# Dealing a weight conversion out over the slots of the first batch, and moving reciprocals one slot later

## The chip, the cores and the metric

The kernel runs on one core of a Trainium2 chip. The metric is the device time of one execution in microseconds (us), taken as the median of several runs. Engines are named as in the profile: PE is TensorE (matmuls and transposes), PEld its weight loads, DVE is VectorE, ACT is ScalarE, POOL is GpSimd, SP is SyncE (DMA issue). L405 is line 405 of the kernel.

## The reference

Attention with a threshold, followed by a two-layer network with an exact GELU. There are 8 batches of 8 heads, 576 tokens and 64 elements a head; the network has a width of 512 and 2048 hidden units.

```python
scores = scale * np.matmul(q, k.transpose(0, 1, 3, 2))
thresh = np.max(scores, axis=-1, keepdims=True) - tau
scores = np.where(scores >= thresh, scores, -1000000000.0)
scores = scores - np.max(scores, axis=-1, keepdims=True)
attn = np.exp(scores)
attn = attn / (np.sum(attn, axis=-1, keepdims=True) + 1e-09)
attn_out = np.matmul(attn, v)
...
x = attn_out.transpose(0, 2, 1, 3).reshape(B * S, H * D)
h = x @ w_in
g = 0.5 * h * (1.0 + erf(h * inv_sqrt2))
return g @ w_out
```

q, k and v are float32. The two weights are float64 and reach the kernel as 64-bit words, so that the kernel must make float32 of them by itself.

## The kernel before, in words

**Pairs and slots.** The attention works on pairs of heads, p = 0 to 31, four pairs a batch (`HP`). The 576 rows of a head are cut into four chunks of 128 and one of 64; the last chunks of both heads share one tile. One pair and one chunk make a slot. The list `slots` gives their order, and the main loop at L1050 takes one slot n after another. In the first batch (`BATCH`, slots 0 to 19; `EARLY` is 4 pairs) the order is special: slots 0 to 7 take chunks 0 and 1 of the four pairs, slots 8 to 19 take chunks 2, 3 and 4 of pair 0, then of pair 1, and so on. So slots 10, 13, 16 and 19 are the last, half-sized chunks.

**Order.** The schedule is manual. Every engine executes its own instructions in the order in which the program emits them[...]. What the loop emits earlier stands earlier in the queue of its engine.

**A slot of the first batch** emits, in this order:

- `scores` (L393): four or eight matmuls into two PSUM tiles `sc`. There are only two such tiles, so the scores of a slot wait until L424 of the slot before has read them.
- `softmax_head`: for each head, the negated maximum `nmx` (DVE, L405), the threshold `thr` (POOL, L406), the exponential `p` (ACT, L408).
- `turn_qk_early` in slots 0, 2 and 4: transposes of the next pair's q and k (PE L309), copied by ACT.
- `weigh_v` and `divide_early` for what is in `due`: p x v (PE, L527), its copy (ACT, L537); the reciprocal sums spread to columns by matmul (PE, L446), their copy (ACT, L448), the product on POOL (L454). `due` holds chunks of earlier slots, two slots late at the soonest.
- `fill`: matmuls of the network's first layer (PE, L603), from slot 10 on, as many as a fixed goal for each slot asks; `need > converted[0]` holds back those whose weights are not yet converted.
- `turn_p_early` of the slot before: transposes of p (PE, L339), copied by ACT (L346, L355; L350, L359 for the last chunk). For a last chunk this comes after the next item but one.
- `convert(0, least)`: at least one step of the conversion, up to 700 ns of steps where i is 4.
- `softmax_tail`: threshold, product and row sums (DVE, L424), and 1e-9 added to the sums (POOL, L427).
- transposes of q and k for the second batch in slot 17 (`turn_qk`, L375 to L381; the q there is scaled by ACT, L363).
- `convert(ns)`: steps of the conversion worth ns.
- `invert`: the reciprocal of the slot's sums (DVE, L433), which waits for L427.

**The conversion.** The weights come in 32 pieces of 128 x 512 numbers. For each piece ACT makes two values (L201, `power`; L202) and DVE takes three steps (L209, L211, L214), booked by the generator `conversions` at 340, 720 and 640 ns. A piece's two ACT instructions are emitted when an earlier piece ends, so that up to two pieces are `ahead`. `convert` keeps a debt: it adds ns and takes steps until the debt is used up. The end of a piece also issues the load of another piece (L183, on POOL). The raw words lie in tiles that are used by the attention only later (`turned_p`) and in free slots of `xall`.

The main loop gives

```python
convert(0 if n == 0 else 2000 if n < 3 else 3800 if n < BATCH - 1 else 1e9)
if early:
    invert(p, i)
```

which is 2000 ns in slots 1 and 2, 3800 ns in slots 3 to 18, and all that is left in slot 19. The 32 pieces are booked at 54.4 us in all.

**After the first batch** the attention of the other batches runs in the same loop, with its own way of transposing p on DVE, and with more of the network filled in between; then the last ten blocks of 256 tokens are done by `last_blocks`. None of this is touched.

Of the kernel before, what the change touches and what calls it, by code (L numbers as in the profile page):

```python
# [18 lines left out]
def kernel(  # L19
# [37 lines left out]
    EARLY = HP  # L57
# [128 lines left out]
    def conversions():  # L186

        vec = nc.vector
        ahead = []
        while raws or ahead:
            if raws:
                dst, raw, slot = raws.pop(0)
                lo, hi = (raw.rearrange("p (f w) -> p f w", w=2)[:, :, i] for i in range(2))
                power = gp.tile([P, PIECE], U32, tag="g", name="power")  # L200
                nc.scalar.activation(power.bitcast(FP32), hi.bitcast(FP32), AF.Copy, bias=0.0, scale=2.0 ** -112)  # L201
                nc.scalar.activation(dst.bitcast(U32), lo, AF.Copy, bias=0.0, scale=2.0 ** -29)  # L202
                ahead.append((dst, hi, power, slot))
                yield 0
            if len(ahead) == LATER and converted[0] == len(pieces) - LATER:
                yield None
            if len(ahead) == 2 or not raws:
                dst, hi, power, slot = ahead.pop(0)
                vec.tensor_scalar(power, power, 3, 0x7FFFFFF8, op0=ALU.logical_shift_left, op1=ALU.bitwise_and)  # L209
                yield 340  # L210
                vec.scalar_tensor_tensor(power, hi, 0x80000000, power, op0=ALU.bitwise_and, op1=ALU.bitwise_or)  # L211
                x_free.extend(slot)
                yield 720
                vec.tensor_tensor(dst.bitcast(U32), power, dst.bitcast(U32), op=ALU.add)  # L214
                load_piece()
                converted[0] += 1
                yield 640
# [3 lines left out]
    def convert(ns, least=0):  # L221

        if conv["steps"] is None:
            conv["steps"] = conversions()
        conv["debt"] += ns
        while conv["debt"] > 0 or least > 0:
            took = next(conv["steps"], None)
            if took is None:
                return
            conv["debt"] -= took  # L230
            least -= took
# [152 lines left out]
    def scores(p, i):  # L384
        s = st[p]
        n = 1 if i == NC else 2
        sc = s["sc", i] = [ps.tile([P, 2, 512], FP32, tag="sc", name="sc", bufs=2) for _ in range(n)]
        for h in range(2):
            for e in range(n):
                rows = slice(0, P) if i == NC else slice(e * D, (e + 1) * D)  # L390
                lhsT = s["q_tail"] if i == NC else s["qT"][rows, i * P:(i + 1) * P]
                at = h * HALF + (TAIL if p < EARLY and e == 0 else 0)
                nc.tensor.matmul(  # L393
                    sc[e][:, h, 0:HALF], lhsT=lhsT, rhs=s["kT"][rows, at:at + HALF], start=True, stop=True)

    def softmax_head(p, i):

        s = st[p]
        n = len(s["sc", i])
        nmx = small.tile([P, 2], FP32, tag="nmx", name="nmx")  # L400
        thr = s["thr", i] = small.tile([P, 2], FP32, tag="thr", name="thr")
        w = s["p", i] = work.tile([P, 2 * S], FP32, tag="p", name="p")
        for e in range(n):
            sc = s["sc", i][e][:, :, 0:HALF]
            nc.vector.tensor_reduce(nmx[:, e:e + 1], sc, axis=AXIS.XY, op=ALU.max, negate=True)  # L405
            nc.gpsimd.tensor_scalar(  # L406
                thr[:, e:e + 1], nmx[:, e:e + 1], -1.0, tau_eff, op0=ALU.mult, op1=ALU.subtract)
            nc.scalar.activation(  # L408
                w[:, e * S:(e + 1) * S].rearrange("p (h s) -> p h s", h=2), sc, AF.Exp, bias=nmx[:, e:e + 1], scale=1.0)
# [20 lines left out]
    def invert(p, i):  # L430

        den = st[p]["sum", i]
        nc.vector.reciprocal(den, den)  # L433
# [129 lines left out]
    def gelus(left):  # L563


        while len(late) > left:
            g, j, hT = late.pop(0)
            t = gp.tile([P, 2, TOK], FP32, tag="g", name="g")
            if hold[0]:
                nc.scalar.copy(t, hT)  # L570
                held.append((g, j, t))
            else:
                gelu(g, j, t, hT)
# [107 lines left out]
    def weights_first():  # L681
        room = tail["room"] = early_end.enter_context(tc.tile_pool(name="wsum", bufs=1, side="right", reuse_waits="tile"))
        tail["s"] = room.tile([P, 4, 2, 2, P], FP32, name="s_out")
        tail["ss"] = room.tile([P, 4, 3, P], FP32, name="s_in")
        tail["sp"] = room.tile([P, 3, 4, P], FP32, name="s_plain")
        tail["t"] = room.tile([P, 4, 2, HD], FP32, name="t_out")
        w_in_sums(vec, 0)
# [338 lines left out]
    BATCH = HP * SLOTS  # L1026
# [23 lines left out]
    for n in range(len(slots) + WEIGH + 1):  # L1050
        p, i = slots[n] if n < len(slots) else divmod(n, SLOTS)
        early = p < EARLY
        last = slots[n - 1] if 0 < n <= len(slots) else None
        if p < NP:
            scores(p, i)
            softmax_head(p, i)
            if p < HP - 1 and i == 0:
                turn_qk_early(p + 1)
        elif n == len(slots):
            early_end.close()  # L1060
            weights_first()
        gelus(0)
        if n == BATCH:
            gelus_held()
        table()
        for args in due:
            weigh_v(*args)
            divide_early(*args)
        due = []
        if p > EARLY and i == WEIGH:  # L1070
            for lo, hi in (0, WIDE), (WIDE, S):
                weigh_v(p - 1, lo, hi)
            if p == NP:
                divide(p - 1)
        owed += (goal(n) - goal(n - 1)) * BLK_NS * (PARTS[i] if not early and p < NP else 1.0)
        if early:
            fill(owed, tokens)
            owed = 0.0
            table()
        if last and last[0] < EARLY and last[1] < NC:  # L1080
            turn_p_early(*last)
        if early and n > 2:
            convert(0, 700 if i == NC else 1)
        if p < NP:
            softmax_tail(p, i)
        if p < NP and not early:
            turn_p(p, i)
        if p < NP and not early:
            if i == 2:
                regroup(p, 1)  # L1090
            if i > 2:
                regroup(p, i)
            if i == NC:
                divisors(p)
        if last and last[0] < EARLY and last[1] == NC:
            turn_p_early(*last)
        if p < 2 and i == 0:
            for _ in range(2):
                load_piece()
            load_v_early(p + 2)  # L1100
        if p == 1 and i == NC:
            load(HP)
        if n == BATCH - 3:
            load(HP + 1)
        if n == BATCH:
            for t in pd_tail + [turned_p[:, e, h, :, :] for e in range(2) for h in range(2)]:
                nc.gpsimd.memset(t[:, NB:4 * KR, :], 0.0)
        if EARLY < p < NP and i == DIVIDE:
            divide(p - 1)
        if p >= HP and i == 1 and p + 2 < NP:  # L1110
            loads = load_steps(p + 2)
        if p >= HP:
            next(loads, None)
        if p >= HP and i == 1 and p + 1 < NP or p == HP - 1 and i == 2:
            scale_q(p + 1)
        if p >= HP - 1 and i == 2 and p + 1 < NP:
            turn_qk(p + 1)
        convert(0 if n == 0 else 2000 if n < 3 else 3800 if n < BATCH - 1 else 1e9)
        if early:
            invert(p, i)  # L1120
        if not early:
            lag[0] = 2 if p < NP else 0
            fill(owed, tokens)
            owed = 0.0
        if last and last[0] < EARLY:
            if last[1] == 1:
                due.append((last[0], 0, TOK))
            if last[1] == NC:
                due.append((last[0], TOK, S))
        if n == START - 1:  # L1130
            tokens = TOK
        elif n == BATCH + 1:
            tokens = S
        elif p > EARLY and i == DIVIDE and p % HP == 0 or p == NP and i == WEIGH:
            tokens = p // HP * S
            leaving += [n for n in AWAY if n in x_blk and (n + 1) * TOK <= tokens]
        elif leaving and i < 2:
            put_away(leaving.pop(0))
# [35 lines left out]
```

## Time and profile before

| what | value |
|---|---|
| time, median of 3 runs | 1361.46 us (1360.8 to 1361.97) |
| span of the profiled run | 1358.2 us |
| mean granted clock of PE | 0.991 |
| first batch (start of slot 0 to start of slot 20) | 9.33 to 143.56 us |
| conversion: L209, L211, L214 on DVE | 32 each, from 17.4 us on |
| L201 and L202 on ACT | 32 each, 0.69 us median for L201 |
| reciprocals L433 | 20, 0.158 us median |

The page cuts the span into 40 slices of 34 us; a digit is the busy share of a slice in tenths. The start of a slot is read from the first L405 of that slot on DVE. "Idle before" is the time for which an engine waited ahead of an instruction, with the instruction whose end released it. The chain of waits follows the work that ended last back to what released each step.

### The profile page before, as it was taken

To read this page: it belongs to the slowest core of one execution; us is meant where nothing else is said; L and a number is where in the kernel's file an instruction comes from. 1 tells how busy PE (TensorE), PEld (TensorE's weight loads), DVE (VectorE), ACT (ScalarE), POOL (GpSimd) and SP (SyncE) were. 2 spreads that over 40 slices of the span, in tenths; PEclk is the share of its full clock that TensorE was granted. 3 is DMA by queue.
4 is the path that set the end of the run, shared out by engine and by line. 5 is a ranking of instruction groups with operands and counts; after the bars stand their busy time and mean duration, and the time that the engine had idled before them with its cause. 6 is when DMAs were issued, how large, how long until landed. Compare 5 with 4: busy or idle time off the path is not lost.

```text
span 1358.2 us, 19815 instructions
## 1 busy us (share of the span) xinstructions
PE 1324.9 (98%) x6282; PEld 892.0 (66%) x6282; DVE 1056.6 (78%) x2029; ACT 606.5 (45%) x1027; POOL 620.1 (46%) x1065
## 2 busy tenths in 40 slices
PE   8699899999999999999999999999999999999998
PEld 6466457557457557557557557568787787877877
DVE  6987487788888888888888888875658598385775
ACT  7866537537547537637637636513201112211120
POOL 4432345455456555555555552135363513625530
PEclk9899999999999999999999999999999999999999
DMA  8742267677777777787788777500000041000003
GB/s 269 195 142 50 52 135 174 138 164 176 168 169 181 164 188 186 154 207 179 153 197 191 152 171 160 124 9 1 0 1 0 3 122 32 1 1 0 1 1 78
DMA packets 209782, 152.40 MB, mean 112 GB/s; under 512 B 113360, under 2 KB 193088, under 8 KB 209680
## 3 DMA queue, kind: packets, MB, share of 16 engines
q1 hardware_dynamic: 188224, 112.53, 37.3%
q0 software_dynamic: 21024, 38.32, 10.2%
q8 instruction: 51, 0.84, 0.2%
q14 instruction: 51, 0.42, 0.1%
q10 hardware_dynamic: 432, 0.30, 0.1%
HBM read 55.97 MB, written 12.52 MB: 50 GB/s over the span
## 4 chain that ended last, share of the span: by engine, by line
PE 90%; DVE 4%; ACT 3%; DMA 2%; issue 1%; SPq 0%; POOL 0%; DVEq 0%; ACTq 0%; POOLq 0%
PE bank L791 33%; PE o_ps L618 17%; PE hT L603 15%; PE sc L393 13%; PE xT L527 11%; DVE nmx L405 1%; ACT p L408 1%; DMA x<-xall 1%; DVE p L424 1%; DVE power L211 1%; ACT pT L346 1%; PE tr L339 0%; DVE power L209 0%; DMA v<-in_v_dram 0%; ACT power L201 0%
## 5 line engine op out<-in xcount | busy, mean ns | idle before, releaser
L408 ACT ACTIVATE p<-sc,nmx 128x576 f32<-128x576 f32 x288 | 202.2, 739 | 289.6 <-DVE nmx L405 289.4
L424 DVE SCALAR_TENSOR_TENSOR p<-sc,thr,p 128x576 f32<-128x576 f32 x288 | 225.3, 816 | 66.2 <-ACT p L408 61.8
L406 POOL TENSOR_SCALAR thr<-nmx,tau_eff 128x1 f32<-128x1 f32 x288 | 87.8, 305 | 381.3 <-DVE nmx L405 380.4
L405 DVE TENSOR_REDUCE nmx<-sc 128x1 f32<-128x576 f32 x288 | 205.1, 749 | 53.6 <-PE sc L393 52.7
L618 PE MATMUL o_ps<-w_out,g 128*128 128x512 f32 x512 | 238.7, 606 | 4.0 <-ACT g L576 4.0
L603 PE MATMUL hT<-xall,w_in 128*128 128x256 f32 x1024 | 241.8, 385 | 0.0
L603 PEld LDWEIGHTS hT<-xall,w_in 128*128 128x128 f32 x1024 | 189.4, 190 | 50.0 <-issue 23.0
L673 DVE TENSOR_TENSOR c<-c,bank 128x320 f32<-128x320 f32 x304 | 147.3, 488 | 33.7 <-PE bank L791 20.1
L673 DVE TENSOR_TENSOR o<-o,bank 128x256 f32<-128x256 f32 x240 | 99.9, 420 | 93.7 <-PE bank L791 88.7
L393 PE MATMUL sc<-kT,qT 64*128 64x288 f32 x960 | 163.0, 434 | 9.5 <-DVE p L424 8.8
L527 PE MATMUL xT<-pT,v 128*64 128x256 f32 (+1 forms) x1280 | 169.1, 419 | 0.1
L618 PEld LDWEIGHTS o_ps<-w_out,g 128*128 128x128 f32 x512 | 93.6, 191 | 114.0 <-issue 107.2
L488 DVE STREAM_TRANSPOSE turned_p<-p 128x1152 f32<-128x1152 f32 x112 | 154.4, 1378 | 3.9
L393 PEld LDWEIGHTS sc<-kT,qT 64*128 64x128 f32 x960 | 92.6, 188 | 85.1 <-issue 72.0
L527 PEld LDWEIGHTS xT<-pT,v 128*64 128x64 f32 x1280 | 91.3, 141 | 76.6 <-issue 19.0
L791 PE MATMUL bank<-w_out,c 128*128 128x256 f32 x480 | 120.2, 381 | 0.5 <-DVE o L673 0.5
L259 POOL DMA_DIRECT2D v<-in_v_dram x208 | 110.8, 536 | 3.9 <-issue 2.1
L791 PEld LDWEIGHTS bank<-w_out,c 128*128 128x128 f32 x480 | 89.9, 190 | 18.8 <-DVE o L673 3.0
L844 ACT ACTIVATE c<-c 128x320 f32<-128x320 f32 (+1 forms) x80 | 46.9, 624 | 114.6 <-DVE c L673 114.5
L791 PE MATMUL bank<-t_out,c 128*128 128x256 f32 x320 | 82.7, 381 | 0.0
L791 PE MATMUL bank<-t_out,g 128*128 128x256 f32 x320 | 82.1, 379 | 0.0
L673 POOL TENSOR_TENSOR c<-c,g 128x320 f32<-128x320 f32 (+1 forms) x40 | 50.5, 1272 | 67.5 <-DVE c L673 67.5
(179 smaller groups left out, 1741.6 us busy)
## 6 DMA issues: line engine op xcount, KB each, us to landing
pT<-turned_p SPq DMA_DIRECT2D x448, 160.0 KB, 3.6
pT<-pd_tail SPq DMA_DIRECT2D x112, 80.0 KB, 3.0
q<-in_q_dram POOLq DMA_DIRECT2D x104, 72.0 KB, 3.5
k<-in_k_dram POOLq DMA_DIRECT2D x104, 72.0 KB, 3.3
inv<-turned SPq DMA_DIRECT2D x54, 128.0 KB, 4.1
v<-in_v_dram POOLq DMA_DIRECT2D x156, 40.0 KB, 3.2
out_dram<-o SPq DMA_DIRECT2D x40, 128.0 KB, 2.4
xall<-in_moe_w_out_dram POOLq DMA_DIRECT2D x9, 512.0 KB, 3.9
```

The source lines that it names most:

```text
L259: eng.dma_start(t[r:P:4, e, 0:n, :], rows[:, r * KR:r * KR + n, :])
L393: nc.tensor.matmul(sc[e][:, h, 0:HALF], lhsT=lhsT, rhs=s["kT"][rows, at:at + HALF], start=True, stop=True)
L405: nc.vector.tensor_reduce(nmx[:, e:e + 1], sc, axis=AXIS.XY, op=ALU.max, negate=True)
L406: nc.gpsimd.tensor_scalar(thr[:, e:e + 1], nmx[:, e:e + 1], -1.0, tau_eff, op0=ALU.mult, op1=ALU.subtract)
L408: nc.scalar.activation(w[:, e * S:(e + 1) * S].rearrange("p (h s) -> p h s", h=2), sc, AF.Exp, bias=nmx[:, e:e + 1], scale=1.0)
L424: nc.vector.scalar_tensor_tensor(row, sc[e][:, :, 0:HALF], thr[:, e:e + 1], row, op0=ALU.is_ge, op1=ALU.mult, accum_out=den[e])
L488: nc.vector.transpose(turned_p[:, :, i // 2, 0:NB, i % 2 * Q:(i % 2 + 1) * Q], w.rearrange("p (e b i) -> p e b i", e=2, i=Q))
L527: nc.tensor.matmul(to, lhsT=s["v"][:, e, c, :], rhs=rhs, start=(c == 0), stop=(c == KR - 1))
L603: nc.tensor.matmul(hT[:, j % 2, :], lhsT=w_in_sb[c][:, j * P:(j + 1) * P], rhs=x_blk[n][:, c, :], start=(c == 0), stop=(c == N_DM - 1))
L618: nc.tensor.matmul(o[:, 0:d_model], lhsT=g[j][:, m * P:(m + 1) * P], rhs=w_out_sb[j], start=(j == 0), stop=(j == N_DF - 1))
L673: eng.tensor_tensor(out, a, b, op=ALU.add)
L791: nc.tensor.matmul(to, lhsT=l, rhs=r, start=start and k == 0, stop=k == len(pairs) - 1, skip_group_check=not start)
```

## The change

The conversion's share in slots 3 to 18 goes from 3800 to 3100 ns: 2 x 2000 + 16 x 3100 = 53.6 us of the booked 54.4, so that the conversion reaches into slot 19 instead of ending in slot 16. It is for an even load of DVE over the batch.

The reciprocal of a slot's sums is emitted one slot later, after the next slot's `softmax_head`. It is for not holding DVE up at the end of a slot, where the reciprocal waits for POOL.

```diff
@@ -1054,6 +1054,8 @@
         if p < NP:
             scores(p, i)
             softmax_head(p, i)
+            if last and last[0] < EARLY:
+                invert(*last)
             if p < HP - 1 and i == 0:
                 turn_qk_early(p + 1)
         elif n == len(slots):
@@ -1115,9 +1117,7 @@
             scale_q(p + 1)
         if p >= HP - 1 and i == 2 and p + 1 < NP:
             turn_qk(p + 1)
-        convert(0 if n == 0 else 2000 if n < 3 else 3800 if n < BATCH - 1 else 1e9)
-        if early:
-            invert(p, i)
+        convert(0 if n == 0 else 2000 if n < 3 else 3100 if n < BATCH - 1 else 1e9)
         if not early:
             lag[0] = 2 if p < NP else 0
             fill(owed, tokens)
```

## The prediction

> **What bounds the kernel now.** I read first the page's engine line and its slices, then the windows of the slots of the first batch (cut at the first nmx, L405, of each slot), then the chain of waits and the engines' timelines there.
>
> ```profile
> PE 1324.9 (98%) x6282; PEld 892.0 (66%) x6282; DVE 1056.6 (78%) x2029; ACT 606.5 (45%) x1027; POOL 620.1 (46%) x1065
> PE   8699899999999999999999999999999999999998
> DVE  6987487788888888888888888875658598385775
> ```
>
> TensorE is full from the third slice on, except in the first four slices (34 us each), which hold the first batch; there VectorE is at 9 and 8. So the change can only act in the first 144 us, and what it saves there the rest, a sequence of the same work, keeps.
>
> ```profile
> 47.82:54.75 6.93, 4.04 (x14) 2.55 (x16) 6.83 (x16) 4.93 (x10) 3.16 (x6) 0.69 0.42 132
> 61.90:69.05 7.15, 4.26 (x15) 2.58 (x17) 6.91 (x16) 5.32 (x10) 2.66 (x6) 0.65 0.63 218
> 82.89:89.21 6.32, 4.35 (x23) 2.46 (x23) 6.22 (x15) 4.74 (x10) 2.38 (x5) 0.90 0.57 184
> 89.21:100.33 11.12, 10.88 (x63) 8.10 (x62) 7.09 (x16) 6.35 (x13) 3.79 (x7) 0.90 0.31 94
> 124.77:132.02 7.25, 7.25 (x45) 4.95 (x45) 4.83 (x13) 3.72 (x8) 1.13 (x4) 1.00 0.09 20
> 132.02:138.82 6.80, 6.51 (x46) 5.25 (x43) 3.13 (x8) 3.88 (x9) 1.84 (x5) 1.00 0.11 27
> ```
>
> Columns: window, length, busy PE, PEld, DVE, ACT, POOL, granted clock, DMA share, GB/s. The rows are slots 6, 8, 11, 12, 17 and 18. Up to slot 11 VectorE is busy for all of a slot and TensorE is not; from 12 on TensorE is, and slots 17 and 18 leave VectorE 2.4 and 3.7 us free, since the conversion ended in slot 16. That is uneven dealing.
>
> ```profile
> 50.71 2.99 PE sc L393 x8
> 53.70 4.09 PE xT L527 x20
> 57.80 0.44 PE tr L446 x8
> 58.23 0.60 PE tr L339 x4
> 58.91 1.07 ACT pT L346 x2
> 60.15 0.58 ACT power L201
> 60.76 0.44 DVE power L209
> ```
>
> ```profile
> 50.71 2.99 PE L393 MATMUL sc<-pd_tail,qT 64*128 64x288 f32 x8 [4.38 <-DVE p L424]
> 64.79 3.00 PE L393 MATMUL sc<-kT,qT 64*128 64x288 f32 x8 [3.12 <-DVE p L424]
> 85.77 1.94 PE L393 MATMUL sc<-kT,qT 64*128 64x288 f32 x8 [1.95 <-DVE p L424]
> 109.01 1.94 PE L393 MATMUL sc<-pd_tail,qT 64*128 64x288 f32 x8 [1.31 <-DVE p L424]
> ```
>
> But the chain does not run on VectorE alone: in slot 7 it goes scores, p x v, transposes on TensorE, their copy and a power (L201) on ScalarE, then L209. TensorE had waited 4.38 us for VectorE and ran slowly: eight score matmuls took 2.99 us against 1.24 in slot 8.
>
> **What the Trainium skill says.** TensorE: Matmul & The Clock Gate, Part 1 (the HAM clock gate): an idle window of about 3.4 us halves the clock and a busy one restores it. The trace agrees: windows of 2 us show 0.50 from 51 to 57, from 65 to 69 and at 89 to 91, each after TensorE idled or worked little. SBUF — State Buffer, two separate sides: a VectorE operation with two SBUF inputs and a GpSimd operation exclude each other; here L211 and L214 take 1.11 to 1.13 us instead of 0.69 beside L454 on GpSimd. This stays. Perfetto Trace Analysis, Tensor Engine Instruction: ScalarE and VectorE are strict first in, first out; the waits below rest on that.
>
> **The change, part by part.** *Reciprocals.* Twenty of 0.158 us, but the next L405 starts 0.07 us after one starts, so 0.07 each, and they stay. Behind the reciprocal on VectorE stands only the next L405. It waited for GpSimd (L427) in slots 0, 15, 18, 19: 0.36, 1.24, 1.67, 0.42 us; after each, VectorE waited again for the next scores (0.41, 0.93, 1.80, 1.69), so that removing the first waits is worth about nothing. After the change a reciprocal stands behind the next two L405, in the 0.2 us in which L424 waits for the exponential, or before a conversion step; L424 and the scores behind it wait at most 0.07 us. Its reader, L446, comes a slot later. I take 0.
>
> *Conversion.* The same 96 steps (L209, L211, L214) are dealt differently. The order of VectorE's instructions gives, up to the L424 of slot 11, 63 steps before and 52 after: 11 fewer. From rows in a run without waits (86.28 to 88.08: three steps in 1.80 us), a step costs 0.58 to 0.60, so 6.4 us leave the stretch that VectorE bounds. They go to slots 12 to 19.
>
> Now the walk, each slot from its own steps: two L405 1.32 us, reciprocal 0.07, two L424 1.47, L209 0.45, L211 0.7, L214 0.6.
> Slot 3 loses one step: slot 4 starts at 31.7 (before 32.52). Slot 4 has five steps for seven, and its L209 no longer waits 0.95 us for a power queued in the same slot (38.73): 5.9 us, slot 5 at 37.6 (40.70). Slot 5, six steps, one beside L454: 6.5, slot 6 at 44.1 (47.82). Slot 6, six steps: 6.3, slot 7 at 50.5 (54.75).
> Slot 7 is where gain is lost. VectorE would be at its second L209 at 55.4. That L209 needs a power queued behind the pT copies of this slot, which need p x v. TensorE's chain starts at the end of slot 6's L424, 47.4 (before 50.5), and takes 10.05 us (50.71 to 60.76) if the clock is low again; TensorE still idles some 3.7 us, so I take it as low. L209 comes at 57.6, a wait of 2.2 instead of 0.32 us, and slot 8 starts at 58.7 (61.90): 3.2 gained, not 5.3. Slot 8, six steps: slot 9 at 65.0 (69.05). In slot 9 the same: scores at 61.65, plus 9.84 us (64.79 to 74.63), L209 at 71.5. But only this L209 is left before slot 10, no longer an L211 and an L214: slot 10 at 71.9 (76.60). Slot 10, five steps for eight: 4.8, slot 11 at 76.7 (82.89). Its L424 end at 80.0, so the scores of slot 12 start at 80.1 instead of 85.77: 5.7 us gained. The check by sums: 6.4 for steps, plus waits of 0.95, 0.32 and 0.61 us gone, minus 2.2 and 0.8 us new, is 5.3.
> TensorE then idled 0.4 us in place of 1.95 before those scores, having just worked for 7 us, so I take its clock as full in slot 12: p x v takes 2.9 in place of 4.6 us. That is 1.7 more; with the scores (1.94 before, as the second head's waited for its L424; 1.24 now) the gain grows from 5.7 to 8.0.
>
> From here TensorE is the bound: slots 12 to 19 have 3.2 us of idle in all. Its fixed matmuls take what they took, while VectorE has 11 steps more. The walk finds: L209 of slot 15 waits about 2 us for a power behind that slot's pT copies and delays slot 16's L405 by 0.8, which fill L603 (2.75 us) covers; slot 15's scores wait 1.8 us where before they waited 1.31. Slot 17 gets six steps: its qT transpose still waits on L363, then 3.1 us of steps follow, so slot 18 starts at 126.0 instead of 132.0, while TensorE is 8.9 early; L424 of slot 18 ends at 129.1, just as TensorE comes to the next scores (128.8). In slot 19 an L214 before L424 costs 0.6. So I book nothing gained or lost in 12 to 19 beyond 8.0; slot 20's scores end at 135.2 to 135.5 instead of 143.58.
>
> *After slot 20.* All is converted in both, in the same order of TensorE's matmuls, and transfers move with the slots. ScalarE only trades places of L201 and L202. So 1361.46 - 8.0 = 1353.5 us.
>
> **The rivals.** *A, more gain.* The clock stays full in slots 7 and 9, since TensorE idles 3.7 instead of 4.38 us. Each loses some 3.3 us at half clock now (6.5 us at 0.50); the wait of 2.2 us in slot 7 then goes, and 0.8 in slot 9, and some of it at 12: 1350.0. Against: slot 9's scores were slow after only 3.12 us of idle. *B, less gain.* The clock in slot 12 stays low (loses 1.7 to 2.3), and 17 to 19 add 2 us, as a step there now stands in front of L424 on which scores wait: 8.0 - 2.2 - 2 = 3.8, 1357.7. For it: slot 18 has no slack in my walk. *C, no change.* TensorE and ScalarE's queue take all: slots 7 and 9 give back all their gain and 15 to 18 the rest, 1361.5. Against: slots 3 to 6, 10 and 11 show VectorE nearly gapless. *D, slower.* Nothing is gained before 12 and the 11 steps, 6.4 us, lie open in 12 to 19 save the 2.4 us free in slot 17: 1361.5 + 4.0 = 1365.5. Against: 17 and 18 show 6.1 us free.
>
> **How the numbers follow.** Forecast 0.50, A 0.14, B 0.20, C 0.08, D 0.08. The range from A's 1350.0 to 1357.6, just within B, leaves out about 2 in 10: C, D, the far half of B or a further A. Faster by over 0.2% (below 1358.7) takes forecast, A and almost all of B: 0.83; same 0.08; slower 0.09.
>
> **What would show it right or wrong.** Right: slot 12's scores near 80, clock 1.00 in slot 12, L405 of slot 20 near 135.5, L209 of slot 7 waiting 2 us for L201, conversion to slot 19, and all after shifted by one amount. Wrong: 0.50 clock at slot 12; L393 waiting over 1 us for L424 in 18 to 20 (B); L405 of slot 12 not early (C); or a shift at slot 20 that the end does not show.

## The result, and the profile after

| | before | after |
|---|---|---|
| time, median of 4 runs | 1361.13 us (1360.74 to 1361.97) | 1356.03 us (1353.57 to 1356.18) |
| ratio | | 0.9957 (95%: 0.9940 to 0.9975) |
| span of the profiled run | 1358.2 us | 1354.4 us |
| slot 0 to slot 12, first L405 to first L405 | 79.9 us | 74.1 us |
| slot 0 to slot 18 | 122.7 us | 117.0 us |
| slot 0 to slot 20 | 134.2 us | 129.3 us |

The kernel became 5.1 us faster by the medians; 1353.5 was forecast, 8.0 faster. In the profiles the batch is 4.9 us shorter from slot 0 to slot 20, which is nearly all of it. Slot 0, ahead of anything that was changed, starts 0.4 us later in this profile (9.73 for 9.33), so below I count from slot 0 where two profiles are set side by side.

The page after; the first four digits of each row cover the first batch.

```profile
PE 1324.7 (98%) x6282; PEld 893.0 (66%) x6282; DVE 1057.1 (78%) x2029; ACT 605.7 (45%) x1027; POOL 623.0 (46%) x1065
PE   8799899999999999999999999999999999999998
DVE  6987677788888888888888888875758598385775
```

TensorE's second digit went from 6 to 7. VectorE has 6, 9, 8, 7, 6 where it had 6, 9, 8, 7, 4. The fifth slice (136 to 170 us) holds no conversion before and 0.7 us of it after; it is busier because the second batch, which begins in it, comes earlier. The even dealing itself does not show in VectorE's digits. The work is the same. The windows of the same six slots (6, 8, 11, 12, 17, 18; length, then PE, PEld, DVE, ACT, POOL, granted clock, DMA share, GB/s) show where it went:

```profile
45.15:51.58 6.43, 3.74 (x12) 2.34 (x14) 6.22 (x15) 4.79 (x9) 2.47 (x6) 0.70 0.46 142
59.00:65.32 6.32, 3.36 (x10) 2.10 (x12) 6.22 (x14) 5.37 (x11) 2.46 (x5) 0.69 0.48 156
77.36:83.78 6.42, 6.27 (x37) 4.09 (x37) 6.21 (x15) 4.74 (x10) 2.55 (x6) 1.00 0.60 184
83.78:92.08 8.30, 8.00 (x53) 6.50 (x50) 6.04 (x14) 5.55 (x13) 3.69 (x7) 1.00 0.47 149
116.82:126.68 9.86, 9.86 (x65) 7.00 (x63) 8.07 (x18) 5.89 (x12) 1.29 (x4) 1.00 0.10 28
126.68:135.48 8.80, 6.17 (x25) 4.97 (x25) 6.33 (x13) 5.08 (x11) 2.60 (x5) 0.81 0.01 3
```

Slots 6 and 8 went from 6.93 and 7.15 to 6.43 and 6.32 us. Slot 12 went from 11.12 to 8.30 us, at clock 1.00 instead of 0.90. Slots 17 and 18 together went from 14.05 to 18.66 us, and in 18 TensorE is idle for 2.6 us and its clock falls to 0.81. That idle is new. TensorE's timeline of the kernel after shows what it waits for (start, length, line, what, idle before and its releaser):

```profile
47.84 3.00 PE L393 MATMUL sc<-pd_tail,qT 64*128 64x288 f32 x8 [3.71 <-DVE p L424]
61.96 2.99 PE L393 MATMUL sc<-kT,qT 64*128 64x288 f32 x8 [3.10 <-DVE p L424]
80.05 1.94 PE L393 MATMUL sc<-kT,qT 64*128 64x288 f32 x8
100.35 1.94 PE L393 MATMUL sc<-pd_tail,qT 64*128 64x288 f32 x8 [0.74 <-DVE p L424]
124.78 1.99 PE L603 MATMUL hT<-xall,w_in 128*128 128x256 f32 x8
129.40 1.90 PE L603 MATMUL hT<-xall,w_in 128*128 128x256 f32 x4 [2.63 <-ACT g L570]
```

The fill of slot 18, twelve records of L603 (the trace shows two records for each of these matmuls), stops after eight and waits 2.63 us for L570. In the kernel before, the same twelve ran through:

```profile
133.46 2.86 PE L603 MATMUL hT<-xall,w_in 128*128 128x256 f32 x12
```

The last four now take 1.90 us, where a third of these 2.86 would be 0.95. ScalarE's timelines say why L570 is late, first the kernel before, then the kernel after:

```profile
132.79 1.41 ACT L408 ACTIVATE p<-sc,nmx 128x576 f32<-128x576 f32 x2 [2.00 <-DVE nmx L405]
134.10 0.58 ACT L570 COPY g<-hT 128x512 f32<-128x512 f32 x1
```

```profile
127.47 1.41 ACT L408 ACTIVATE p<-sc,nmx 128x576 f32<-128x576 f32 x2 [3.91 <-DVE nmx L405]
128.77 0.58 ACT L570 COPY g<-hT 128x512 f32<-128x512 f32 x1
```

L570 copies the first layer's sums out of one of four PSUM buffers and so frees it. It needs nothing from slot 18, but it is emitted behind slot 18's exponentials. These wait 3.91 us for L405, and L405 was late because VectorE had five conversion steps at the end of slot 17. Before, L570 started 0.6 us after the fill had begun; now it starts 4.0 us after.

### The profile page after: what moved, and what is told of

It reads as the page before. It is cut to its first block, busy times and chain, and to the rows that moved or that the text cites. A ratio compares the mean times of both kernels' runs of the same rounds, so it can differ in the third digit from the quotient of the medians.

```text
span 1354.4 us, 19808 instructions
## 1 busy us (share of the span) xinstructions
PE 1324.7 (98%) x6282; PEld 893.0 (66%) x6282; DVE 1057.1 (78%) x2029; ACT 605.7 (45%) x1027; POOL 623.0 (46%) x1065
## 4 chain that ended last, share of the span: by engine, by line
PE 88%; ACT 1%; DVE 1%; DMA 0%; issue 0%; POOL 0%; SPq 0%; DVEq 0%; POOLq 0%; ACTq 0%
PE bank L791 34%; PE o_ps L618 17%; PE hT L603 15%; PE sc L393 12%; PE xT L527 10%; DMA x<-xall 0%; ACT p L408 0%; DVE nmx L405 0%; PE tr L339 0%; DVE p L424 0%; POOL xall L551 0%; ACT L576 0%; SPq L476 0%; ACT g L570 0%; DVE o L673 0%
## 5 line engine op out<-in xcount | busy, mean ns | idle before, releaser
L424 DVE SCALAR_TENSOR_TENSOR p<-sc,thr,p 128x576 f32<-128x576 f32 x288 | 225.3, 816 | 66.1 <-ACT p L408 63.6
L603 PE MATMUL hT<-xall,w_in 128*128 128x256 f32 x1024 | 242.8, 386 | 2.6 <-ACT g L570 2.6
L405 DVE TENSOR_REDUCE nmx<-sc 128x1 f32<-128x576 f32 x288 | 205.3, 750 | 50.8 <-PE sc L393 49.6
L618 PE MATMUL o_ps<-w_out,g 128*128 128x512 f32 x512 | 239.5, 608 | 3.8 <-ACT g L576 3.8
L603 PEld LDWEIGHTS hT<-xall,w_in 128*128 128x128 f32 x1024 | 189.6, 190 | 53.1 <-issue 23.0
L618 PEld LDWEIGHTS o_ps<-w_out,g 128*128 128x128 f32 x512 | 94.0, 192 | 114.4 <-issue 107.8
L673 POOL TENSOR_TENSOR c<-c,g 128x320 f32<-128x320 f32 (+1 forms) x40 | 50.5, 1271 | 67.5 <-DVE c L673 67.5
```

The source lines that it names most:

```text
L424: nc.vector.scalar_tensor_tensor(row, sc[e][:, :, 0:HALF], thr[:, e:e + 1], row, op0=ALU.is_ge, op1=ALU.mult, accum_out=den[e])
L603: nc.tensor.matmul(hT[:, j % 2, :], lhsT=w_in_sb[c][:, j * P:(j + 1) * P], rhs=x_blk[n][:, c, :], start=(c == 0), stop=(c == N_DM - 1))
L618: nc.tensor.matmul(o[:, 0:d_model], lhsT=g[j][:, m * P:(m + 1) * P], rhs=w_out_sb[j], start=(j == 0), stop=(j == N_DF - 1))
L673: eng.tensor_tensor(out, a, b, op=ALU.add)
```

## The experiments

**Which half of the change.** Each alone, against the kernel before; first the rate:

```diff
-        convert(0 if n == 0 else 2000 if n < 3 else 3800 if n < BATCH - 1 else 1e9)
+        convert(0 if n == 0 else 2000 if n < 3 else 3100 if n < BATCH - 1 else 1e9)
         if early:
             invert(p, i)
```

> The new rate of 3100 ns alone, reciprocals at the end of their own slot as before. If the whole gain is the dealing (the prediction's sum, reciprocals worth 0): 1356, as with the whole change, within 0.7. If the reciprocals carry a part, as they no longer hold VectorE up behind GpSimd: 1357.5 to 1359.

Measured: 1355.61 us, ratio 0.9962 (0.9949 to 0.9974). Then the reciprocals, with 3800 kept:

```diff
             softmax_head(p, i)
+            if last and last[0] < EARLY:
+                invert(*last)
...
         convert(0 if n == 0 else 2000 if n < 3 else 3800 if n < BATCH - 1 else 1e9)
-        if early:
-            invert(p, i)
```

> The moved reciprocals alone, the rate of 3800 ns as before. If they are worth nothing, since VectorE waits for scores behind each of the four waits anyway: 1361, within 0.7 of the kernel before. If they carry a part: 1358.5 to 1360.

Measured: 1359.65 us, ratio 0.9992 (0.9984 to 1.0001). So the dealing alone gives the whole gain. The reciprocals alone lie between nothing and 2.2 us; that interval touches both expectations, the median lies within the second, and what they bring alone stays open. Beside the dealing they bring nothing that shows, as 1355.61 and 1356.03 say. The traces have no common sign: counted from slot 0, the moved reciprocals bring slot 7 0.9 us earlier at 3800 ns and 0.8 us later at 3100. At 3800 slot 12 is 2.3 us earlier, but most of this is made in slots 7 and 9, where p x v took 3.13 and 3.45 us instead of 4.16 and 3.95; a low clock of another length is a rival here that one trace does not settle. The wait of L433 for GpSimd is gone as meant (3.7 us in four waits before, none after).

**The loss in slot 18.** L570 ahead of the exponentials:

```diff
             scores(p, i)
+            if early:
+                gelus(0)
             softmax_head(p, i)
```

> The whole change, and in the first batch the copies of the first layer's sums (L570) are emitted ahead of the exponentials of the slot instead of behind them. Theory: slot 18 loses 2.6 us of TensorE idle and then some 1.7 us at half clock because L603 waits for a PSUM buffer that L570 frees, and L570 stands behind an exponential that waits for a late L405. Then L603 waits no more in slot 18, the clock stays full, and the time is 4 lower than with the change: 1352. Rival: VectorE itself is late in slots 17 to 19, and the next scores would wait for L424 in any case: then the idle moves from L603 to L393 and the time stays at 1356, within 1.

Measured: 1352.58 us, ratio 0.9935 (0.9921 to 0.9948), against 0.9957 of the change. The intervals overlap, but all five runs lie below the fastest of the change. ScalarE's timeline of this kernel:

```profile
122.20 0.59 ACT L570 COPY g<-hT 128x512 f32<-128x512 f32 x1
126.09 1.41 ACT L408 ACTIVATE p<-sc,nmx 128x576 f32<-128x576 f32 x2 [3.31 <-DVE nmx L405]
127.40 0.48 ACT L537 COPY xall<-xT 128x256 f32<-128x256 f32 x2
```

and TensorE's:

```profile
123.88 2.86 PE L603 MATMUL hT<-xall,w_in 128*128 128x256 f32 x12
127.93 1.09 PE L339 MATMUL tr<-ident,p 128*128 128x128 f32 x8 [1.20 <-ACT xall L537]
```

The exponential still waits 3.31 us for a late L405, but the twelve L603 run through. Of the 2.63 us of idle 1.20 is left, now at L339, for a buffer that L537 frees, which still stands behind the exponential; the clock stays at 1.00. The rival, that the next scores would wait for L424 instead, is out: the scores of slot 19 wait for nothing.

The same from the other side: no conversion at the end of slot 17, so that L405 itself is early.

```diff
-        convert(0 if n == 0 else 2000 if n < 3 else 3100 if n < BATCH - 1 else 1e9)
+        convert(0 if n in (0, BATCH - 3) else 2000 if n < 3 else 3100 if n < BATCH - 1 else 1e9)
```

> The whole change, but slot 17 takes no conversion at its end (one step before L424 stays); its share goes to slots 18 and 19, where six steps then stand behind L424 of slot 19. Theory: L405 of slot 18 comes 3 us earlier, so exponential and L570 too, and L603 in slot 18 does not wait; but slot 20's L405 now waits about 1 us for the last steps: 2.8 lower than with the change, 1353.3. Rival (the loss lies in VectorE's total load of 17 to 19, wherever it stands): 1356, within 1.

Measured: 1352.60 us, ratio 0.9944 (0.9932 to 0.9957). The median is 3.4 us below the change, but one of the five runs (1355.60) lies among those of the change, so that here the trace is the stronger evidence. No idle of over 0.3 us is left on TensorE in slots 18 and 19, and slot 18 starts 3.4 us earlier, counted from slot 0. As expected the price is paid in slot 20: VectorE comes out of its six last steps at 136.28, TensorE had the scores ready at 134.2, and the first L618 waits 6.02 us instead of 3.75.

The third way leaves all in place but lets the five steps of slot 17 run while VectorE waits for L363:

```diff
-        if p >= HP - 1 and i == 2 and p + 1 < NP:
-            turn_qk(p + 1)
         convert(0 if n == 0 else 2000 if n < 3 else 3100 if n < BATCH - 1 else 1e9)
+        if p >= HP - 1 and i == 2 and p + 1 < NP:
+            turn_qk(p + 1)
```

> The whole change, but in slot 17 the conversion's five steps stand ahead of the transposes of q and k, where VectorE waits 1.65 us for L363, instead of behind them. Theory (slot 18's loss hangs on when its L405 comes): L405 1.65 earlier, L603 waits 1.0 instead of 2.6 us, 1354.4; if TensorE's clock then stays full, 1.7 more: 1352.7. Rival (the loss comes from the number of steps, not their place): 1356, within 0.7.

Measured: 1355.37 us, ratio 0.9960 (0.9947 to 0.9972): by the time alone, the rival's value. The trace says more. The mechanism is as the theory says: L603 waits 0.97 us instead of 2.63, its last four take 1.13 us, and counted from slot 0 the first L618 of slot 20 starts 3.1 us earlier (130.9 for 134.0). But then that group is slower. TensorE's timeline there, first of the kernel with the change, then of this one:

```profile
143.74 6.00 PE L618 MATMUL o_ps<-w_out,g 128*128 128x512 f32 x10 [3.75 <-ACT g L576]
```

```profile
140.29 7.44 PE L618 MATMUL o_ps<-w_out,g 128*128 128x512 f32 x10 [3.57 <-ACT g L576]
```

The same ten records take 1.44 us more. In both kernels TensorE has just idled for over 3.5 us, waiting for the first GELUs. That is not the whole account: at slot 24 the trace of this kernel is 2.5 us ahead of the other's, counted from slot 0, but its profiled run was only 1.45 us faster (1354.73 for 1356.18). The mechanism in slot 18 is shown; where the time goes afterwards is only in part. This asked for a test of the clock.

**The clock.** First slots 6 and 8, where TensorE waits for L424 ahead of the slow scores of 7 and 9:

```diff
         if last and last[0] < EARLY and last[1] < NC:
             turn_p_early(*last)
+        if n in (6, 8):
+            hot = ps.tile([P, 2 * P], FP32, tag="mm", name="hot")
+            for _ in range(12):
+                nc.tensor.matmul(hot[:, 0:P], lhsT=ident, rhs=ident, start=True, stop=True)
```

> The whole change, with twelve idle 128x128 matmuls (their result is not used) in slots 6 and 8, where TensorE waits 3.7 and 3.1 us for L424. If the low clock in slots 7 and 9 holds the gain back there, as the prediction has it: eight scores take 1.2 instead of 3.0 us and p x v 2.9 instead of 4.2 and 4.0, the waits of L209 for L201 (1.74 us in slot 7, 0.66 in slot 9) go, slot 12 comes 2.4 earlier, and the time is 1353.6, 2.4 below the change. Rival: VectorE bounds these slots alone, the slow matmuls are hidden: 1356, within 0.7, though the matmuls are faster.

Measured: 1352.87 us, ratio 0.9936 (0.9922 to 0.9949).

```profile
43.95 2.84 PE L1087 MATMUL hot<-ident 128*128 128x128 f32 x24
47.83 1.94 PE L393 MATMUL sc<-pd_tail,qT 64*128 64x288 f32 x8 [1.03 <-DVE p L424]
49.70 2.38 PE L527 MATMUL xT<-pT,v 128*64 128x256 f32 x20
```

p x v of slot 7 takes 2.38 us instead of 4.21, and slot 12 starts 70.9 us after slot 0 instead of 74.1. So the low clock did hold the gain back, by 3.1 us in the trace rather than 2.4. Is that a property of the change, or was it so before? The same lines in the kernel before:

> The kernel before, with the twelve idle matmuls in slots 6 and 8. If VectorE bounds slots 3 to 11 there, with only 0.32 and 0.61 us of waits for L201 in slots 7 and 9, a full clock brings at most these 0.9 us: 1360.0. Rival (the low clock costs the kernel before as much as the changed one): 1357.7, 3.2 lower.

Measured: 1362.07 us, ratio 0.9998 (0.9988 to 1.0008). By the times the gain is at most 1.6 us, which excludes the rival's 3.2 and allows the 0.9 of the first expectation. That would fit a VectorE that needs those slots anyway and hides the slow matmuls, so that the change laid them bare. But the trace of this run does not agree: slots 7 and 9 are 0.8 us shorter each than in the kernel before, and counted from slot 0, slot 12 comes 1.5 us earlier and slot 20 3.2 (131.0 for 134.2). The rest of the 3.2 comes from slot 12, where no idle matmul stands; its p x v ran fast this time, after the same wait of 1.95 us:

```profile
85.87 2.91 PE L527 MATMUL xT<-pT,v 128*64 128x320 f32 x20
```

The profiled run was the fastest of the thirteen (1358.32), so it does not stand for all of them. What the low clock costs the kernel before stays open: nothing that the times show, 1.5 us up to slot 12 of one trace.

**All together.**

> The change with all three: L570 ahead of the exponentials, idle matmuls in slots 6 and 8, conversion ahead of the transposes in slot 17. If their gains lie in different stretches and add up: 1352.6 (L570 first) less 2.4 (clock) less 1.2 (the wait of L339 for L537 that is left in slot 18) = 1349.0. If L570 first and the earlier steps mend the same wait and nothing is left for the second: 1350.2.

Measured: 1349.66 us, ratio 0.9914 (0.9900 to 0.9927). The median lies between the two expectations and does not decide. The trace says that the gains add up: counted from slot 0, slot 20 comes 7.3 us earlier than with the change, where L570 first brought 3.3 and the idle matmuls 3.1, and in slot 18 no wait of over 0.3 us is left. Then fourteen idle matmuls more in slot 20 (`if n == BATCH:`, after `turn_p_early` of the last chunk):

> As the one with all three, with fourteen more idle matmuls in slot 20, where TensorE waits 3.6 to 4 us for the first GELUs. Theory: after that wait the clock is low for a time[...], ten L618 take 6.0 to 7.6 us instead of 4.3, and this makes the runs of one kernel differ by 2 to 3 us. Then the ten take about 4.3 us, the time is 1347.5 (1.5 to 3 lower), and the runs lie within about 1 us. Rival: the spread comes from elsewhere: 1349.7, spread as before.

Measured: 1345.86 us, ratio 0.9880 (0.9865 to 0.9895).

```profile
132.06 3.29 PE L1108 MATMUL hot<-ident 128*128 128x128 f32 x28
135.78 4.56 PE L618 MATMUL o_ps<-w_out,g 128*128 128x512 f32 x10 [0.43 <-ACT g L576]
```

The ten L618 take 4.56 us, where they took 6.22 without the fourteen. Of the 3.8 us between the medians (1349.66 and 1345.86) this is 1.7 in the traces. Another 1.6 lies in slot 21: there, behind the same wait of 1.58 us, the kernel without the fourteen ran eight scores and ten L618 at a low clock (5.76 us the L618 alone), and this one did not (4.56). Whether the fourteen matmuls did that too, or chance, is not shown; other kernels without them had 4.56 there. The four runs lie within 0.94 us (1345.55 to 1346.49), those of the kernel without these fourteen, also four, within 2.88, and the 17 of the kernel before that were measured beside it within 5.9 (1358.60 to 1364.53). This is the fastest version of the study, 15.7 us below the kernel before.

**The rate.** 3400 instead of 3100:

> The whole change with a rate of 3400 ns: 57 steps up to L424 of slot 11, where 3100 has 52 and 3800 has 63, and the conversion ends in slot 17, with four steps behind the transposes there instead of five. If each step taken out of the stretch that VectorE bounds is worth 0.58 us: slot 12 comes 2.9 later than with the change, slot 18 waits about as before, 1358.5. Rival (the gain comes from not bunching, and a middle rate does as well or better since less is left for slots 17 to 19): 1355 to 1356.

Measured: 1354.57 us, ratio 0.9953 (0.9941 to 0.9966): near the rival's 1355 to 1356, far from 1358.5, and no difference to 3100 that can be told. Slot 12 comes only 0.7 us later than with 3100, counted from slot 0 (74.7 for 74.1), not 2.9. In slot 7 the extra steps fall into the time in which VectorE, with 3100, waits 1.74 us for L201; that wait isn't there with 3400. So a step is worth 0.58 us only in a slot that VectorE bounds, and after the change slot 7 is no longer such. In slot 18 L603 waits 1.19 us instead of 2.63, which more than pays back what is lost: slot 20 comes 1.6 us earlier than with 3100 in the traces.

## Why the prediction was right, and where it was off

*Direction and place.* Right: the gain comes from VectorE's relief in slots 3 to 11, and what is left of it after slot 18 the later work nearly keeps.

*Reciprocals at 0.* Not contradicted, and not shown for the reciprocals alone; see their interval above.

*The walk to slot 12.* Counted from slot 0, so that the later start drops out, the slots came earlier by (predicted in brackets): 7: 3.6 (4.3), 8: 3.3 (3.2), 9: 4.1 (4.1), 10: 4.7 (4.7), 11: 5.9 (6.2). The scores of slot 12 came 6.1 us earlier (5.7). The step on slot 7 is the one that kept this sum from being larger: its second L209 waits for a power queued behind slot 7's own copies.

```profile
57.93 0.43 DVE L209 TENSOR_SCALAR power<-power 128x512 uint32<-128x512 uint32 x1 [1.74 <-ACT power L201]
```

A wait of 1.74 us was measured; 2.2 was predicted. The walk let TensorE's chain start at the end of both L424 of slot 6, 3.3 us after that slot's start, but the 50.5 that it set beside this was the end of the first; the scores wait for the first only, and started 2.7 us after. The clock in slots 7 and 9 was low, as the forecast and not rival A had it: 3.00 and 2.99 us for eight scores.

*Slot 12 at full clock.* Right, first the kernel before, then the kernel after; slot 13 came 8.7 us earlier, counted from slot 0.

```profile
87.65 4.60 PE L527 MATMUL xT<-pT,v 128*64 128x320 f32 x20
81.92 2.91 PE L527 MATMUL xT<-pT,v 128*64 128x320 f32 x20
```

But the 1.7 us of this term depend on which run of the kernel before was profiled. With the idle matmuls in slots 6 and 8 that kernel took 2.91 us here too, after the same wait of 1.95 us for L424. How often its slot 12 runs at the low clock is not known.

*Slots 12 to 19, "I book nothing gained or lost in 12 to 19 beyond 8.0".* This step failed. (Its sum of TensorE's idle there, 3.2 us, is 3.0 in the windows; that changes nothing.) Up to the fill of slot 17 the gain was kept and more: that fill starts at 116.00 instead of 125.13, 9.1 earlier, helped by slot 15, whose scores waited 0.74 us where the walk had 1.8. Then slot 18 gave back 4.1: its fill starts 8.7 us earlier (124.78 for 133.46), the scores behind it 4.6 (133.10 for 137.65). The walk had slot 18's VectorE time right (L405 predicted at 126.0, measured 126.68) and asked only who waits for L424. It did not follow the other reader of L405, the exponential, to what stands behind it on ScalarE: the copy that frees TensorE's buffer. The term was set at 0 and measured 4.1, of which 2.63 are idle and the rest mostly low clock. In the traces, counted from slot 0 to slot 20, the run with L570 ahead won 3.3 us of it back and the one with no steps in slot 17 2.4; by the medians both won 3.4.

*After slot 20.* Nearly right: the lead of 4.9 us at slot 20 is 4.2 at the end of the two profiles. The kernel after lost 1.6 us in slot 21 at a low clock, which the last section shows; kernels with the new rate had both a low and a full clock there.

*Rival B* (3.8 us gained) is nearer to the measured 5.1 than the forecast's 8.0. It named slots 17 to 19 as the place of a loss, which is where it lay, but with the wrong cause: a step in front of L424, and scores waiting for it. Its other half, a low clock in slot 12, did not come. So the mechanism up to slot 17 was right. That the total came as near as it did, although a loss of 4.1 us had been left out, is in part luck: the gain up to slot 17 was larger than booked.

## What to carry to other kernels

When work is moved into a slot that has room on one engine, follow every reader of the instruction that becomes late, and on each reader's engine ask what is queued behind it: here a copy with no tie to the late data held a PSUM buffer and stopped the matmuls. Emit copies that free buffers ahead of instructions that wait for something else. And when the bounding engine is relieved, look at what ran slowly beneath it unseen: a low clock on TensorE cost the changed kernel 3 us here. What it cost the kernel before is not settled, though no gain could be measured in its time.

## What the runs showed of the hardware that was not expected

TensorE's clock fell after less idle than the prediction took from the Trainium skill (TensorE: Matmul & The Clock Gate, Part 1: an idle window of about 3.4 us). In the kernel after, 2.63 us of idle in slot 18 were followed by a granted clock of 0.50 from 131 to 133 us; in the run with L570 ahead, 1.20 us were not. The kernel before had one such place already, which the prediction counted as agreement: 0.50 from 89 to 91 us, after 1.95 us of idle within four microseconds (83 to 87) of which TensorE was busy for 2.0.

Nor does the same wait always have the same effect. In slot 21 TensorE waits 1.58 us for L424 in every kernel of this study. Here are the kernel before and then the kernel after:

```profile
167.34 1.94 PE L393 MATMUL sc<-kT,qT 64*128 64x288 f32 x8 [1.58 <-DVE p L424]
169.22 4.56 PE L618 MATMUL o_ps<-w_out,g 128*128 128x512 f32 x10
```

```profile
162.61 2.61 PE L393 MATMUL sc<-kT,qT 64*128 64x288 f32 x8 [1.58 <-DVE p L424]
165.14 5.54 PE L618 MATMUL o_ps<-w_out,g 128*128 128x512 f32 x10
```

From 164 to 166 us the clock of the kernel after was 0.50. Of the twelve traces five have this loss and seven do not. What decides it is not shown. A difference of 1.6 us between two single profiles can therefore not be put down to the edit here.

Keeping TensorE busy with idle matmuls through waits that it has anyway brought 3.2 us in slots 6 and 8 with the change, by the medians, and 1.7 us in slot 20, by the traces. Most of the spread between runs of one kernel went with the last: 0.9 us for 2.9, with four runs each.
